# An RWKV attention fused into a cosine feed-forward: the end of the first order, the source of two chunks' bonus sums, the place of the decays' check and the lag of the last units

## The chip, the cores and the metric

One Trainium2 chip, one of its cores. The metric is device microseconds (us) of one execution; the profile is of one further execution of the same program.

## The reference, cut to what matters

```python
def _attn_ref(r, k, v, w, u):          # (4, 8, 768, 48) each, u (8, 48)
    for t in range(S):
        cur = einsum('bhd,bhe->bhde', u * k[t], v[t])
        y[t] = einsum('bhd,bhde->bhe', r[t], state + cur)
        state = w[t][..., None] * state + einsum('bhd,bhe->bhde', k[t], v[t])
def _moe_ref(x, w_in, w_out):          # x (3072, 384), w_in (384, 2048), w_out (2048, 384)
    h = x @ w_in
    return (h * cos(h)) @ w_out
```

The attention's output, with its heads side by side, is x.

## The kernel before, in words

**Tiling.** The sequence is cut into 24 chunks of 128 steps, numbered in the order of work: chunks 0 to 3 are the first chunk of each of the four batches, 4 to 7 the second, and so on. Two chunks make a block, so there are 12 blocks. The feed-forward of a block is 8 units (`NU`), each of two 128-wide pieces of the 2048. There are 96 units (`slots`), and t counts them. Blocks 0 and 1 share t = 0 to 15 in a mixed order; from t = 16 on, block 2 has t = 16 to 23, block 10 t = 80 to 87, block 11 t = 88 to 95.

**A unit.** `mm1(t)` is 18 matmuls on TensorE into a PSUM bank `ph`. Then comes the gate: I (ScalarE, L402), S (VectorE, L405), N (the sine on ScalarE, L418), M (VectorE, L419, the last reader of `ph`), H (ScalarE, the rounded high part, into `gs`), L (GpSimd, the low part, L145, in two halves). `mm2(t)` is 12 matmuls that read `gs` and add to the block's sums. `LAG` is 2: mm2(t-2) stands behind mm1(t). `gs` has two buffers, and while blocks 0 and 1 are both open `ph` has two banks (h0, h1) and all else on TensorE two (a0, a1).

**A block of attention.** For each chunk: loads (`load`, `lr` for r and k as they lie in memory, `lv`), the decay's two scans and products on VectorE (`decay`: e, f, r, k), the bonus sum (`diag`), which GpSimd's affine_select places on a diagonal (`asb`), the scores (`a`, written into `asb` by copy_predicated, P), the transposes of k (`t`, copied out as `kn`, K), the state (`s`, `d`), the own products (`o`), the products with the past (`p`) and their split into `xT` (X: xh on ScalarE, then x on VectorE), which mm1 of that block reads and which frees the two banks of `o`.

**Bonus sums.** Below chunk `BY_PE` VectorE multiplies r and k (`rkt`, L216), TensorE sums with u (`pc`, L241) and ScalarE copies (`cd`). From `BY_PE` on, `lr` loads r and k, two products are made (m, L247, and u, L248, with `u_sb`), and VectorE sums (c, L252). The engines of m and u come from a table: GpSimd in `EARLY`, VectorE in `LATER`. The buffers of `lr` ("h", two) are those through which the weights pass.

**Order.** `START` is the order for t = 0 to 15. There only TensorE runs in the order as written; the other engines' queues are put in order by a planner that works with estimated durations, and each queue then runs strictly in that order. From t = 16 on TensorE, VectorE, ScalarE and GpSimd run in the order of `PLAN`, whose row t % 8 is read for each t; only SP's queue is planned. `check_decays` (a load of 768 KB, a reduction and a maximum on VectorE) runs `WCH` = 6 times, behind the row of t = 90 to 95. `take_vote` stands behind t = 95: three small VectorE steps and two pairs of small matmuls (`pv`) in TensorE's queue. The program ends with a branch on the vote.

Of the kernel before, what the change touches and what calls it, by code (L numbers as in the profile page):

```python
# [26 lines left out]
NCB = 6  # L27
W129 = NP * 129
BLK = 2
BY_PE = 8  # L30
BT = BLK * C
WCH = 6
IN_PARTS = 2
# [12 lines left out]
LAG = 2  # L46
# [6 lines left out]
PLAN = ["t+2 t+3 load+6 mm1 K+2 K+3 e+4 I S k+4 N M mm2 H L f+4",  # L53
# [12 lines left out]
PAIR = "0001110101010101"  # L66
NEEDS = dict(decay="load", lr="load", lv="load", diag="lr", d="decay", a="decay diag", t="decay",
             o="a lv", s="t d lv", p="o d")
# [3 lines left out]
def rwkv_cos_ffn(ctx: ExitStack, tc: tile.TileContext, tr, tn, tv, u, ut, wts, w, rkw, vst, us, xs, out):  # L72
    nc = tc.nc
# [15 lines left out]
    def bank(kind, shape, name):  # L89

        tags = BANKS[stage[0]]
        turn[kind] += 1
        return ps.tile(shape, F32, tag=tags[kind][turn[kind] % len(tags[kind])], name=name)
# [3 lines left out]
    def buf(tag, shape, dtype, name=None, pool=sb):  # L97
        return pool.tile(shape, dtype, tag=tag, name=name or tag, bufs=BUFS.get(tag, 1))
# [31 lines left out]
    E = {}  # L130
# [49 lines left out]
    by_hand, parts = [False], {}  # L180
# [9 lines left out]
    def att_load(j):  # L190
# [8 lines left out]
        if j == 0:  # L199
            E["qt"].dma_start(out=u_by_head, in_=ut)  # L200
        if j == BY_PE:
            E["qt"].dma_start(out=u_sb, in_=u.to_broadcast([C, DM]))
# [9 lines left out]
    def att_decay(a):  # L212

        if a["j"] < BY_PE:
            a["rkt"] = buf("rkt", [R, NP, C], F32)
# [21 lines left out]
    def att_diag(a):  # L237
        if a["j"] < BY_PE:
            pc = bank("a", [C, 512], "pc")[:, :8]
            for p in range(NP):  # L240
                nc.tensor.matmul(out=pc[:, 2 * p:2 * p + 2], lhsT=a["rkt"][:, p], rhs=u_by_head[:, p], start=True, stop=True)  # L241
            cd = buf("cd", [C, 8], F32)
            copy("cd", cd, pc)
            picked(a, cd)
        else:
            rk = a["rk"][:, 0]
            part(("m", a["j"]), lambda: E["rk"].tensor_tensor(out=rk, in0=rk, in1=a["rk"][:, 1], op=ALU.mult))  # L247
            part(("u", a["j"]), lambda: E["ru"].tensor_tensor(out=rk, in0=rk, in1=u_sb, op=ALU.mult))  # L248

            def sums():  # L250
                cd = buf("cd", [C, 8], F32)
                nc.vector.tensor_reduce(out=cd, in_=rk.rearrange("p (h d) -> p h d", d=HD), axis=mybir.AxisListType.X, op=ALU.add)  # L252
                picked(a, cd)

            part(("c", a["j"]), sums)
# [131 lines left out]
    def check_decays(n):  # L387

        ww = buf("tt", [128, w.shape[1] // WCH], F32, "ww")
        nc.sync.dma_start(out=ww, in_=w[:, n * w.shape[1] // WCH:(n + 1) * w.shape[1] // WCH])  # L390
        top = buf("top", [128, 1], F32)
        nc.vector.tensor_reduce(out=top, in_=ww, axis=mybir.AxisListType.X, op=ALU.max, apply_absolute_value=True)
        nc.vector.tensor_tensor(out=wmax, in0=wmax, in1=top, op=ALU.max)
# [33 lines left out]
    def mm1(t, half=None):  # L427
        i, u = seq[t]
        if not half:
            weights("f", (u + 1) * FU + LEAD + FLEAD)  # L430
            weights("w", (u + 1) * FU + LEAD)
            for j in range(BLK):
                att(i * BLK + j, "x")
            units[t] = bank("h", [C, FU, BT], "ph")
        xT, ph = xts[i], units[t]
        for fi in range(FU) if half is None else (half,):
            n = 0
            for kt in range(KT):
                for a, b in PASSES:
                    nc.tensor.matmul(out=ph[:, fi], lhsT=wgt[u * FU + fi][:, 0, a, kt * 128:(kt + 1) * 128], rhs=xT[:, b, kt],  # L440
                                     start=n == 0, stop=n == 3 * KT - 1)
                    n += 1
        if half is None or half == FU - 1:
            gate(sb, ph, t)
# [35 lines left out]
    NU = NF // FU  # L480
# [3 lines left out]
    for i in PAIR:  # L484
# [3 lines left out]
    slots = len(seq)  # L488
    seen = set()
    n_checked = [0]  # L490
    done = {"f": 0, "w": 0}
    steps = dict(load=None, lr=att_load_rk, lv=att_load_v, decay=att_decay, diag=att_diag, d=att_dstate,
                 a=att_scores, t=att_transpose, s=att_state, o=att_own, p=att_past, x=att_x)

    def att(j, n):

        whole = n in "osp"
        if not 0 <= j < (NBLK if whole else NG) or (j, n) in seen:
            return
        for m in ("decay" if n == "diag" and j < BY_PE else NEEDS.get(n, "")).split():  # L500
            for c in (range(j * BLK, (j + 1) * BLK) if whole and m not in "osp" else (j,)):
                att(c, m)
        i = j // BLK
        if n == "load":
            for m in "osp":
                att((j - BUFS["tt"]) // BLK, m)
        elif n == "t":
            att((j - BUFS["kn"]) // BLK, "s")
        elif n == "d" and j >= NB:
            att(i - SAME, "s")  # L510
            att((j - BUFS["dd"]) // BLK, "s")
            att(i - 1, "p")
        elif n == "lv":
            att((j - BUFS["v"]) // BLK, "o")
            att((j - BUFS["v"]) // BLK, "s")
        elif n == "x":
            att(i, "p")
        seen.add((j, n))
        if n == "load":
            att_load(j)  # L520
        else:
            steps[n](j if whole else atts[j])
# [8 lines left out]
    def up(n):  # L531

        if n == 0 and up1[0] < slots:
            if up1[0] - up1[1] > LAG:
                up(1)
            mm1(up1[0])
            up1[0] += 1
        elif n == 1 and up1[1] < up1[0]:
            mm2(up1[1])
            up1[1] += 1  # L540

    def events(i, row, t):
        for e in row.split():
            n, _, d = e.partition("+")
            if e == "mm1":
                up(0)
            elif e == "mm2":
                if up1[1] <= t - LAG:
                    up(1)
            elif e in "ISNMHL":  # L550
                if (e, t) in parts:
                    parts.pop((e, t))()
            elif n in "efrkmucPKXn":
                at = i * (1 if n in "Xn" else BLK) + int(d)
                for m in dict(e=("decay",), m=("diag",)).get(n, ()):
                    att(at, m)
                if (n, at) in parts:
                    parts.pop((n, at))()
            else:
                att(i * (1 if n in "osp" else BLK) + int(d), n)  # L560

    def take_vote():
        vote = cst.tile([128, 1], F32, name="vote")
        nc.vector.tensor_single_scalar(out=vote, in_=wmax, scalar=1.0, op=ALU.is_gt)
        least = cst.tile([R, 1], F32, name="least")
        nc.vector.tensor_reduce(out=least, in_=wholes.rearrange("p g a -> p (g a)"), axis=mybir.AxisListType.X, op=ALU.min)
        low = cst.tile([R, 1], F32, name="low")
        nc.vector.tensor_single_scalar(out=low, in_=least, scalar=LEAST, op=ALU.is_le)
        pv = bank("a", [C, 512], "pv")
        nc.tensor.matmul(out=pv[:1, 0:1], lhsT=vote, rhs=ones[:, 0:1], start=True, stop=True)  # L570
        nc.tensor.matmul(out=pv[:1, 1:2], lhsT=ones[:R, 0:1], rhs=low, start=True, stop=True)
        votes = cst.tile([1, 1], F32, name="votes")
        nc.vector.tensor_reduce(out=votes, in_=pv[:1, 0:2], axis=mybir.AxisListType.X, op=ALU.add)
        nc.vector.tensor_copy(out=bad, in_=votes)
# [3 lines left out]
    up1 = [0, 0]  # L578
# [13 lines left out]
    engines(LATER)  # L592
    by_hand[0] = True
    with tc.manual_schedule(engines={ET.PE, ET.DVE, ET.Activation, ET.Pool}):
        for t in range(up1[0], slots + LAG):
            events(t // NU, PLAN[t % NU], t)
            if t >= slots - NU + 2 and n_checked[0] < WCH:
                check_decays(n_checked[0])
                n_checked[0] += 1
            if t == slots - 1:  # L600
                take_vote()
    assert not parts, list(parts)

    fast.close()
# [157 lines left out]
```

## Time and profile before

| | |
|---|---|
| median of the runs | 545.68 us |
| profiled execution, its own time | 545.42 us |
| its span, first to last instruction | 543.6 us |
| mean granted clock of TensorE | 0.972 |
| busy: TensorE matmul / weight load | 510.0 / 493.2 us |
| busy: VectorE / ScalarE / GpSimd | 378.3 / 274.1 / 213.5 us |
| HBM over the span | 93 GB/s |

The profiled execution stands 0.26 us below the median, and 1.8 us of its time lie outside its span. Busy shares are means over stages that differ: the weights and blocks 0 and 1 at the start, the even course of blocks 2 to 10, and block 11, which has no attention beside it.

### The profile page before, as it was taken

How to read it: one execution, taken by the hardware profiler on the slowest of the kernel's cores; microseconds unless marked ns; L12 is line 12 of the kernel's file. 1: busy time of each engine (PE TensorE's matmuls, PEld its weight loads, DVE VectorE, ACT ScalarE, POOL GpSimd, SP SyncE). 2: the span in 40 equal slices, each digit the busy share in tenths (PEclk: the TensorE clock that was granted, in tenths of full speed). 3: DMA queues.
4: the chain of work that ended last, by engine and by line, in shares of the span. 5: the costliest groups of instructions: out<-in, count | busy, mean ns of one | idle time of the engine just before them, and what ended most of it. 6: DMA issues, size and time to landing. Idle time of an engine off the chain costs nothing. (4 is left out here: it accounts for less than half of the span.)

```text
span 543.6 us, 11944 instructions
## 1 busy us (share of the span) xinstructions
PE 510.0 (94%) x4980; PEld 493.2 (91%) x4980; DVE 378.3 (70%) x568; ACT 274.1 (50%) x456; POOL 213.5 (39%) x274
## 2 busy tenths in 40 slices
PE   3667999989999999999999999999999999999995
PEld 3656898989999999999999999999999999999984
DVE  7998999954647947947947947947947847433682
ACT  1788999533444444444444444444444444444541
POOL 4161355743233533533533533533533634323331
PEclk9869999988999999999999999999999999999997
DMA  8984851105141150151150151151150130030200
GB/s 274 323 305 137 276 165 60 60 1 137 60 135 32 59 139 27 60 130 38 59 149 19 60 138 31 59 132 34 59 173 2 60 118 0 30 118 1 87 2 32
DMA packets 16440, 51.38 MB, mean 95 GB/s; under 512 B 1984, under 2 KB 8384, under 8 KB 16384
## 3 DMA queue, kind: packets, MB, share of 16 engines
q1 hardware_dynamic: 16240, 50.49, 30.3%
q8 instruction: 40, 0.66, 0.5%
q14 instruction: 16, 0.13, 0.1%
q10 hardware_dynamic: 144, 0.10, 0.1%
HBM read 45.87 MB, written 4.72 MB: 93 GB/s over the span
## 5 line engine op out<-in xcount | busy, mean ns | idle before, releaser
L145 POOL TENSOR_TENSOR gs<-rr,gs 128x256 fp32r<-128x256 f32 x192 | 160.0, 854 | 249.9 <-ACT gs L142 249.9
L440 PE MATMUL ph<-xT,w 128*128 128x256 f32 x1728 | 224.2, 283 | 6.4 <-ACT w L142 4.6
L440 PEld LDWEIGHTS ph<-xT,w 128*128 128x128 f32 x1728 | 215.5, 190 | 9.8 <-ACT w L142 5.1
L459 PE MATMUL acc<-w,gs 128*128 128x384 f32 x1152 | 221.2, 342 | 1.0 <-DVE rr L419 1.0
L459 PEld LDWEIGHTS acc<-w,gs 128*128 128x128 f32 x1152 | 199.9, 191 | 1.8 <-issue 1.4
L405 DVE SCALAR_TENSOR_TENSOR rr<-rr,ph 128x512 f32<-128x512 int32 x96 | 65.5, 683 | 90.9 <-ACT rr L402 90.4
L418 ACT ACTIVATE rr<-rr,quarter 128x512 f32<-128x512 f32 x96 | 69.4, 723 | 85.5 <-DVE rr L405 85.4
L142 ACT CAST gs<-rr 128x512 fp32r<-128x512 f32 x96 | 59.6, 620 | 63.1 <-DVE rr L419 42.4
L419 DVE TENSOR_TENSOR rr<-rr,ph 128x512 f32<-128x512 f32 x96 | 65.7, 684 | 30.2 <-ACT rr L418 30.2
L402 ACT ACTIVATE rr<-ph 128x512 int32<-128x512 f32 x96 | 57.4, 598 | 55.8 <-PE ph L440 55.2
L262 POOL TENSOR_SCALAR_AFFINE_SELECT asb<-cd 128x512 f32<-128x512 f32 x48 | 40.6, 868 | 65.1 <-DVE cd L252 40.9
L222 DVE TENSOR_TENSOR_SCAN ee<-tt,one_e 112x516 f32<-112x516 f32 x24 | 32.1, 1339 | 1.8 <-DMA tt<-tr 1.8
L289 DVE COPY_PREDICATED asb<-mask,pa 128x512 f32<-128x512 uint8 x48 | 31.8, 727 | 2.3 <-PE pa L285 2.3
L229 DVE TENSOR_TENSOR_SCAN tt<-tt,inj 112x516 f32<-112x516 f32 x24 | 30.6, 1276 | 0.6
L145 DVE TENSOR_TENSOR xT<-py,xT 128x384 fp32r<-128x384 f32 x24 | 12.2, 551 | 25.6 <-ACT xT L142 25.6
L285 PE MATMUL pa<-tt 48*128 48x128 f32 x384 | 29.1, 303 | 0.5 <-ACT ob L472 0.5
L285 PEld LDWEIGHTS pa<-tt 48*128 48x128 f32 x384 | 25.8, 208 | 3.6 <-issue 2.2
L241 PEld LDWEIGHTS pc<-u_by_head,rkt 112*128 112x128 f32 x64 | 11.1, 259 | 17.0 <-DVE rkt L216 8.6
L241 PE MATMUL pc<-u_by_head,rkt 112*128 112x2 f32 x64 | 11.4, 300 | 15.8 <-DVE rkt L216 13.4
L234 DVE TENSOR_TENSOR tt<-tt 112x512 f32<-112x512 f32 x24 | 21.6, 898 | 0.0
L142 ACT COPY past<-dd 48x192 f32<-48x192 f32 x40 | 14.0, 350 | 13.4 <-DVE dd L275 13.0
L235 DVE TENSOR_TENSOR tt<-tt,ee 112x512 f32<-112x512 f32 x24 | 19.1, 797 | 0.0
(65 smaller groups left out, 343.9 us busy)
## 6 DMA issues: line engine op xcount, KB each, us to landing
tt<-tr SPq DMA_DIRECT2D x22, 674.2 KB, 6.9
raw<-wts SPq DMA_DIRECT2D x16, 768.0 KB, 5.9
rk<-tn SPq DMA_DIRECT2D x16, 384.0 KB, 3.7
v<-tv SPq DMA_DIRECT2D x24, 224.0 KB, 5.8
ww<-w SPq DMA_DIRECT2D x6, 768.0 KB, 5.2
out<-ob SPq DMA_DIRECT2D x23, 192.0 KB, 2.0
tt<-tr SPq DMA_DIRECT2D x4, 224.0 KB, 4.6
tt<-tr SPq DMA_DIRECT2D x2, 226.2 KB, 3.6
```

Source lines behind the costliest of these rows:

```text
L142: (nc.scalar.copy if E[name] is nc.scalar else E[name].tensor_copy)(out=out, in_=in_)
L145: E[name].tensor_tensor(out=out, in0=full, in1=high.bitcast(F32), op=ALU.subtract)
L222: nc.vector.tensor_tensor_scan(out=ee.rearrange("p a t -> p (a t)")[:, ::-1], data0=wp[:, 1:W129 + 1][:, ::-1], data1=one_e.rearrange("p a ...
L262: nc.gpsimd.affine_select(out=asb, in_=col.unsqueeze(2).to_broadcast([C, NP, C]), pattern=[[0, 4], [1, C]], compare_op=ALU.is_equal, fill= ...
L285: nc.tensor.matmul(out=pa[h][:, p], lhsT=a["k3"][rows(h), p], rhs=a["r3"][rows(h), p], start=True, stop=True)
L289: nc.vector.copy_predicated(a["asb", h], mask, pa[h])
L402: nc.scalar.activation(made["rr"].bitcast(I32), ph, AF.Copy, scale=INV2PI / W_SCALE, bias=0.25)
L405: nc.vector.scalar_tensor_tensor(out=made["rr"], in0=made["rr"].bitcast(I32), scalar=-2.0 * math.pi * W_SCALE, in1=ph, op0=ALU.mult, op1=A ...
L418: N=lambda: nc.scalar.activation(made["rr"], made["rr"], AF.Sin, scale=1.0 / W_SCALE, bias=quarter),
L419: M=lambda: nc.vector.tensor_tensor(out=made["rr"], in0=made["rr"], in1=ph, op=ALU.mult), H=high, L=low)
L440: nc.tensor.matmul(out=ph[:, fi], lhsT=wgt[u * FU + fi][:, 0, a, kt * 128:(kt + 1) * 128], rhs=xT[:, b, kt], start=n == 0, stop=n == 3 * K ...
L459: nc.tensor.matmul(out=accs[i][j][:, :DM], lhsT=gs[:, a, fi, j * C:(j + 1) * C], rhs=wgt[u * FU + fi][:, 1, b], start=u == 0 and fi == 0 a ...
```

## The change

Five things. `BY_PE` falls to 6, so chunks 6 and 7 get their bonus sums from `lr` loads, m, u and c. The last row of `START` is put in another order: transposes of chunks 4 and 5, state of block 2, then its own products and those with the past, with a unit between each. At t = 18 a row of its own (`FIRST`) puts mm1 ahead of the scores of chunks 6 and 7. The decays' check goes to t = 82 to 87 and the vote behind t = 92. The last three units have rows of their own (`LAST`): mm1(94) and mm1(95) follow each other, mm2 lags by 3, H and L stand behind mm2 of the unit that frees their buffer, and L of units 94 and 95 is made by VectorE in one piece.

```diff
-BY_PE = 8
+BY_PE = 6
-         "mm2 m0 m1 o2 p2 mm2 x4 decay6 m0 m1 diag6 lv6 mm2 t4 t5 decay7 m0 m1 mm2 diag7 s2 lv7 lr8 lr9 load8 load9 d6 d7 lv8 lv9"]
+         "mm2 m0 m1 lr6 lr7 diag6 decay6 mm2 t4 t5 m0 m1 lv6 lv7 diag7 decay7 s2 mm2 o2 p2 load8 lr8 lr9 m0 m1 x4 mm2 load9 d6 d7 lv8 lv9"]
+FIRST = {2: "mm1 a+2 a+3 I S m+4 N M P+2 P+3 mm2 H L"}
+LAST = "mm1 I S N M", "mm1 I S N M mm2 h l", "mm2 h l"
+CHECK = 14
@@
-            if up1[0] - up1[1] > LAG:
+            if up1[0] - up1[1] > LAG + 1:
@@
-            elif e in "ISNMHL":
-                if (e, t) in parts:
-                    parts.pop((e, t))()
+            elif e in "ISNMHLhl":
+                at = (e.upper(), t - e.islower())
+                if at in parts:
+                    parts.pop(at)()
@@
-        for t in range(up1[0], slots + LAG):
-            events(t // NU, PLAN[t % NU], t)
-            if t >= slots - NU + 2 and n_checked[0] < WCH:
+        up2 = up1[0]
+        for t in range(up2, slots + LAG):
+            n = t % NU
+            if t == slots - 2:
+                E["g0"] = nc.vector
+            row = FIRST[n] if t < up2 + NU and n in FIRST else PLAN[n]
+            events(t // NU, row if t < slots - 2 else LAST[t - slots + 2] if t <= slots else "mm2", t)
+            if t >= slots - CHECK and n_checked[0] < WCH:
                 check_decays(n_checked[0])
                 n_checked[0] += 1
-            if t == slots - 1:
+            if t == slots - 4:
                 take_vote()
+        while up1[1] < slots:
+            up(1)
```

## Rows read from the trace of the kernel before

**Rows 1.** Windows: busy us and count of each engine, TensorE's clock, DMA, GB/s.
```profile
120.00:140.00 20.00, 19.76 (x154) 19.41 (x155) 9.60 (x16) 8.88 (x19) 6.85 (x10) 0.87 0.40 113
...
250.00:300.00 50.00, 50.00 (x495) 48.85 (x494) 35.80 (x58) 22.77 (x40) 19.75 (x27) 1.00 0.21 62
```

**Rows 2.** Timeline of TensorE, 108 to 142 us: start, us, instruction, idle before it.
```profile
108.90 0.64 PE L352 MATMUL py<-asb,v 128*32 128x128 f32 x16
...
111.82 2.37 PE L459 MATMUL acc<-w,gs 128*128 128x384 f32 x12
...
114.03 2.26 PE L440 MATMUL ph<-xT,w 128*128 128x256 f32 x18
...
118.23 1.86 PE L241 MATMUL pc<-u_by_head,rkt 112*128 112x2 f32 x8 [1.94 <-DVE xT L145]
...
119.96 4.19 PE L459 MATMUL acc<-w,gs 128*128 128x384 f32 x12
...
123.94 1.46 PE L298 MATMUL pt<-ident,tt 112*128 112x112 f32 x8
...
129.45 0.95 PE L241 MATMUL pc<-u_by_head,rkt 112*128 112x2 f32 x8
...
132.58 2.34 PE L440 MATMUL ph<-xT,w 128*128 128x256 f32 x18
...
141.73 2.43 PE L285 MATMUL pa<-tt 48*128 48x128 f32 x32 [0.53 <-ACT ob L472]
```

**Rows 3.** Timeline of the other engines, 96 to 118 us.
```profile
96.07 8.32 SPq L206 DMA_DIRECT2D rk<-tn  x2
...
107.29 2.61 POOL L145 TENSOR_TENSOR gs<-rr,gs 128x256 fp32r<-128x256 f32 x2 [1.94 <-ACT gs L142]
...
109.23 1.76 DVE L229 TENSOR_TENSOR_SCAN tt<-tt,inj 112x516 f32<-112x516 f32 x1
...
112.36 0.69 DVE L419 TENSOR_TENSOR rr<-rr,ph 128x512 f32<-128x512 f32 x1 [0.19 <-ACT rr L418]
...
116.59 0.62 ACT L142 CAST gs<-rr 128x512 fp32r<-128x512 f32 x1 [0.83 <-DVE rr L419]
...
117.11 0.85 ACT L142 CAST xT<-py 128x384 fp32r<-128x384 f32 x2
```

**Rows 4.** Windows of 2 us, columns as in the first group.
```profile
44.00:46.00 2.00, 0.66 (x18) 0.21 (x8) 2.00 (x4) 2.00 (x3) 0.00 (x0) 1.00 0.06 17
...
118.00:120.00 2.00, 1.77 (x9) 1.77 (x9) 1.23 (x3) 0.47 (x1) 0.70 (x2) 0.55 0.00 0
...
534.00:536.00 2.00, 2.00 (x8) 2.00 (x8) 0.00 (x0) 0.00 (x0) 0.00 (x0) 0.50 0.03 8
```

**Rows 5.** Groups by line: shapes, count, busy us, mean ns, idle before.
```profile
L392 DVE TENSOR_REDUCE top<-ww 128x1 f32<-128x1536 f32 x6 | 10.5, 1746 | 0.0
...
L252 DVE TENSOR_REDUCE cd<-rk 128x8 f32<-128x384 f32 x16 | 8.8, 549 | 0.3
...
L216 DVE TENSOR_TENSOR rkt<-tt 112x512 f32<-112x512 f32 x8 | 6.2, 779 | 0.0
```

**Rows 6.** Timeline of all engines, 526 to 540 us.
```profile
526.45 2.25 PE L459 MATMUL acc<-w,gs 128*128 128x384 f32 x12
...
532.53 0.15 DVE L564 TENSOR_SCALAR vote<-wmax 128x1 f32<-128x1 f32 x1
...
533.20 6.65 PE L459 MATMUL acc<-w,gs 128*128 128x384 f32 x24
```

**Rows 7.** Timeline of unit 85 in block 10, 482 to 489 us.
```profile
482.49 2.26 PE L440 MATMUL ph<-xT,w 128*128 128x256 f32 x18
...
485.48 0.69 DVE L405 SCALAR_TENSOR_TENSOR rr<-rr,ph 128x512 f32<-128x512 int32 x1 [2.08 <-ACT rr L402]
...
486.67 2.26 PE L440 MATMUL ph<-xT,w 128*128 128x256 f32 x18
...
486.95 0.69 DVE L419 TENSOR_TENSOR rr<-rr,ph 128x512 f32<-128x512 f32 x1 [0.79 <-ACT rr L418]
```

## The prediction

> **What bounds the kernel now.** First the table of windows over the span. From 250 to 300 us TensorE is busy for all 50.00 us at clock 1.00, and VectorE for 35.80 [rows 1]: the even course is TensorE's, and an edit there gains only what it takes from TensorE. Its reserves lie where it waits or runs at half clock. Two such places touch the change. From 120 to 140 us the mean clock is 0.87 [rows 1]; the other place is the end. So the second view is TensorE's timeline at these places, the third the windows of 2 us for the clock.
>
> At the first place the reader is to see the sums of chunk 6 (`pc`) begin at 118.23 after 1.94 us of idleness, put down to VectorE's `xT` [rows 2]. That is a bank: with two banks for all but gates and sums, `pc` needs one of those in which block 2's own products lie, and X frees them. The products end before 111.82, where mm2(11) begins [rows 2], but X begins at 117.11, since ScalarE's queue has it behind H of unit 13 at 116.59 [rows 3]. Behind the wait the clock is 0.55 [rows 4]; mm2(12) takes 4.19 us instead of the 2.37 of mm2(11) [rows 2].
>
> At the end mm2(93) begins at 526.45, and mm2(94) and mm2(95) only at 533.20: in between TensorE's queue holds the vote's matmuls, and the vote begins at 532.53 [rows 6], behind the last check. Then the 24 matmuls take 6.65 us [rows 6] at clock 0.50 [rows 4].
>
> **The change part by part.** All sums are against the profiled execution (545.42 us, span 543.6); the median is 0.26 us above it.
>
> *First order's end.* The pitch of mm1 and mm2 together is 486.67 - 482.49 = 4.18 us [rows 7], so 2.09 each. What falls away between 108.90, where block 2's own products begin, and mm1(16) at 132.58 [rows 2]:
> - the wait ahead of `pc`: 118.23 - (114.03 + 2.09) = 2.11 us;
> - `pc` of chunk 6: 119.96 - 118.23 = 1.73 us;
> - mm2(12) at half clock: 123.94 - 119.96 = 3.98 instead of 2.09, 1.89 us;
> - the eight transposes at half clock, 1.46 us [rows 2]; at full clock half, so some 0.6 us in the queue (an estimate);
> - `pc` of chunk 7, 0.95 us [rows 2], some 0.9 in the queue.
>
> Together 7.2 us. What comes instead: the products (2.9 us, 108.90 to 111.82) no longer stand between mm1(13) and mm2(11). TensorE now comes to mm1(14) at 108.90 + 2.09 + 0.7 for the transposes = 111.7, and mm1(14) needs the bank of unit 12, whose M begins at 112.36 and ends at 113.05 [rows 3]: a new wait of 1.3 us. Net 5.9 us. Behind it there is room: the state, mm2(12) and the products (2.1 + 2.9 us for the latter two) stand between mm1(14) and mm1(15), and mm1(15) and mm2(13) (4.2 us) between the products and the transposes of chunks 6 and 7, which need X. X then has no late H in front: unit 13's is at 116.59, the products now end near 121.
>
> *Bonus sums.* VectorE loses two `rkt`, 2 x 0.78, and gets two sums, 2 x 0.55 [rows 5]: 0.5 us less. But in `START` m and u are GpSimd's, four instructions of 384 columns. The trace has no such instruction; its nearest row is L with two of 256 columns in 2.61 us [rows 3], so 1.3 to 2 us each, some 6 us, in GpSimd's queue ahead of or between the Ls. Their loads can go no earlier than those of chunks 8 and 9 now: the second of these is issued at 96.07 + 8.32 = 104.39 [rows 3], behind the last weights, which hold the buffer. From below, all this hides in GpSimd's idle times (1.94 us ahead of 107.29 alone [rows 3]) and M of unit 12 comes 0.5 to 1.5 us earlier; from above, M comes 2 us later. I take no shift, as both signs have a row. SP's queue holds `lr8` and `lr9` behind the sums that free their buffers, and behind them the loads of chunk 9, which is wanted only some five units later.
>
> *t = 18.* The scores of chunks 6 and 7 waited 0.53 us for a bank [rows 2]; with mm1(18) ahead that is covered. Gain 0.5 us.
>
> *Check.* A reduction of 1.75 us [rows 5] and a maximum of one column, six times, in VectorE's queue between M and the next S. The maximum lies between 0.15, the vote's step of one column [rows 6], and the 0.69 of a whole M [rows 7]. S of unit 85 stands after 2.08 us of idleness [rows 7], so each check pushes the next S by at most 1.75 + 0.69 - 2.08 = 0.36 us, 2.2 us in all. M(85) ends at 487.64, and its bank is wanted by mm1(87) at 486.67 + 4.18 = 490.85 [rows 7]: 3.2 us of room. So it costs nothing; without that room, up to 2.2 us. At t = 82 four P's stand in the same queue, but there the scores lengthen TensorE's part too. Loads for the check wait in SP's queue with no other load behind them.
>
> *Vote.* Behind t = 92 it stands after M(92). By rows 7, M begins 0.28 us after the next mm1 could; 0.69 for M and 533.20 - 532.53 = 0.67 from the vote to the next matmul [rows 6] make it some 1.6 us late. TensorE waits that long once. Its clock should hold: from 44 to 46 us it was busy for 0.66 of 2.00 us and the clock stayed 1.00 [rows 4].
>
> *Last units.* Gone: 533.20 - (526.45 + 2.09) = 4.66 us of wait, and 6.65 - (2 x 2.09 + 0.16) = 2.31 us of half clock. With lag 3, H(95) waits for mm2(93) and has the 2.09 us of mm2(94) for its own 0.62 [rows 3] and for L on VectorE, which I put at M's 0.69: covered. Net of the vote's wait, 5.4 us.
>
> Sum: 5.9 + 0.5 + 5.4 = 11.8 us; 545.42 - 11.8 = 533.6, and against the median **533.9 us**.
>
> **Rivals.**
> *The gate of unit 12 comes later than now.* M(12) slips by 0.7 us or more, the wait ahead of mm1(14) passes the 1.94 us behind which the clock fell [rows 2], and half clock follows. For it: VectorE is saturated there, and a scan took 1.76 us at 109.23 [rows 3] while L ran on GpSimd. Against it: 0.5 us less VectorE work. Price: a wait of 2.5 us instead of 1.3 and some 3 us of clock (1.89 + 0.6 and part of a unit, as now), so 533.9 + 4.2 = 538.1.
> In its hard form each m and u stops VectorE for its whole length, 6 us; less the 0.5, M comes 5.5 us later, and with the clock's 3 us the time is 533.9 + 8.5 = 542.4. This is what the Trainium skill's page "SBUF — State Buffer", section "Who interferes with whom", would make of it: a VectorE instruction with two SBUF inputs and a GpSimd one that reads SBUF share a port, and the second to issue waits for the first to end. The rows neither bear it out nor rule it out: that scan began at 109.23, when L had 0.67 us to go.
> *X is late again.* The planner puts xh behind another gate, and the wait moves ahead of the transposes of chunks 6 and 7, with the clock behind it: 2.1 + 3 us less, 539.
> *Slower than before.* The two `lr` loads take both "h" buffers before the last two weights do. Then the weights wait for m, u and c, and mm1(14) for the weights of the last unit. It turns slower when that wait exceeds 1.3 + 11.8 - 3 = 10.1 us; with 6 us for m and u and the 8.3 us in which a weight passes its buffer now [rows 3] it is some 14 us, and the time 549.6. Against it: the loads stand behind all weights in `START`.
> *The vote's wait halves the clock* as the longer one does now: 2.3 + some 1 us of it again, 537.
>
> **How the numbers follow.** The forecast 0.60; the gate's late form 0.17, its hard form 0.05; late X 0.09; the vote's clock 0.06; slower 0.03. The range runs from no wait ahead of mm1(14) and 1 us more from earlier waits that shrink with VectorE's load (545.68 - 13.1 - 1.0, near 531.5) to the late forms with a further microsecond, 540; left out are the hard form, the slower case and tails. Two per cent, about what a measurement of this kernel tells from no change, is 534.8: the forecast's own spread (531.5 to 536) has some 0.47 of its 0.60 below that. So faster 0.47, same 0.51, and slower 0.02, since part of the slower case stays within 2%.
>
> **What would show it.** mm1(16) near 126.7 instead of 132.58, no `pc` after chunk 5, and one wait of about 1.3 us ahead of mm1(14) at clock 1.00. The pair of `pv` at t = 92 with 1 to 1.6 us around it. After mm1(95) four mm2 without a gap at clock 1.00, and the last matmul some 11.8 us earlier. No gap in t = 82 to 88. I am wrong if a window between 108 and 127 us shows clock 0.5, if TensorE waits ahead of mm1(14) or t6 for over 2 us, or if `pv` is followed by a low clock.

## The result, and the profile after

The changed kernel takes 538.88 us (median; 538.74 to 538.94), the kernel before 545.54 us beside it: a ratio of 0.9895, with a 95% interval of 0.9867 to 0.9922. One run of the kernel before took 1260.72 us, and the ratio, which is of the fast runs, leaves it out. The gain is 6.7 us by the medians and some 5.7 us by the ratio; 11.8 us were forecast. The time lies inside the stated range of 531.5 to 540 us, but in the part of it that belonged to the rivals. Line numbers are 3 higher than before: M is L422, mm1 L443, mm2 L462, the products m and u L250 and L251, their sum c L255.

The profiled execution took 538.93 us, 6.49 us less than that of before. Its end first. TensorE's timeline of the kernel after:

```profile
513.05 2.25 PE L462 MATMUL acc<-w,gs 128*128 128x384 f32 x12
...
516.24 0.19 PE L574 MATMUL pv<-ones,vote 128*1 128x1 f32 x2 [0.94 <-DVE vote L568]
...
516.70 2.37 PE L443 MATMUL ph<-xT,w 128*128 128x256 f32 x18
...
521.00 4.36 PE L443 MATMUL ph<-xT,w 128*128 128x256 f32 x36
525.20 8.49 PE L462 MATMUL acc<-w,gs 128*128 128x384 f32 x48
```

The reader is to see the last 36 + 48 matmuls without a gap, 8.49 us for 48 where 24 took 6.65 us before [rows 6]. The last ends at 533.69; before it was 533.20 + 6.65 = 539.85 [rows 6]. Of these 6.16 us, 0.84 were already there when block 11 began: its own products start at 474.42 instead of 475.26. So the end is worth 5.3 us. The vote costs 516.70 - (513.05 + 2.09) = 1.56 us, once.

Then the first order's end. TensorE's timeline, 105 to 144 us:

```profile
108.42 2.34 PE L443 MATMUL ph<-xT,w 128*128 128x256 f32 x18 [1.17 <-DVE rr L422]
110.59 2.92 PE L462 MATMUL acc<-w,gs 128*128 128x384 f32 x12
113.36 0.93 PE L301 MATMUL pt<-ident,tt 112*128 112x112 f32 x8
117.48 2.36 PE L443 MATMUL ph<-xT,w 128*128 128x256 f32 x18 [3.19 <-DVE rr L422]
120.46 0.67 PE L323 MATMUL pst<-v,kn 128*64 128x48 f32 x16 [0.62 <-ACT kn L145]
121.90 0.67 PE L323 MATMUL pst<-v,kn 128*64 128x48 f32 x16 [0.78 <-ACT kn L145]
...
132.71 2.35 PE L443 MATMUL ph<-xT,w 128*128 128x256 f32 x18
...
143.36 2.06 PE L288 MATMUL pa<-tt 48*128 48x128 f32 x32
```

All that was to go is gone: no `pc` of chunks 6 and 7 and no half clock (below). Yet mm1(16) stands at 132.71, where it was at 132.58 [rows 2]. mm1(14) begins at 117.48, 4.4 us behind the 113.05 at which the forecast's new wait was to end. In place of what went there are four waits, 1.17 + 3.19 + 0.62 + 0.78 = 5.8 us, and mm2(11), which holds TensorE until 113.36, 0.7 us beyond its 2.09. The two long waits are put down to M (L422). Windows of the kernel after, columns as in rows 1:

```profile
100.00:120.00 20.00, 15.35 (x113) 13.88 (x110) 13.24 (x18) 6.22 (x12) 12.34 (x13) 1.00 0.21 61
120.00:140.00 20.00, 18.76 (x248) 17.91 (x249) 11.47 (x20) 10.76 (x22) 8.87 (x12) 1.00 0.40 114
...
450.00:500.00 50.00, 50.00 (x466) 48.98 (x466) 35.98 (x47) 22.30 (x37) 16.53 (x24) 1.00 0.16 56
```

From 100 to 120 us TensorE works for 15.35 of 20 us, VectorE for only 13.24: the engine on which M runs is not full, it stands. The row of 450 to 500 us, where the check now lies, is full for TensorE. VectorE's timeline says at what it stands:

```profile
104.38 0.55 DVE L255 TENSOR_REDUCE cd<-rk 128x8 f32<-128x384 f32 x1 [2.03 <-POOL rk L251]
...
108.20 1.22 DVE L225 TENSOR_TENSOR_SCAN ee<-tt,one_e 112x516 f32<-112x516 f32 x1
111.35 0.55 DVE L255 TENSOR_REDUCE cd<-rk 128x8 f32<-128x384 f32 x1 [1.93 <-POOL rk L251]
111.82 0.17 DVE L230 RECIPROCAL inj<-ee 112x4 f32<-112x4 f32 x1
111.91 1.48 DVE L238 TENSOR_TENSOR tt<-tt,ee 112x512 f32<-112x512 f32 x1
113.31 1.22 DVE L232 TENSOR_TENSOR_SCAN tt<-tt,inj 112x516 f32<-112x516 f32 x1
114.57 0.69 DVE L237 TENSOR_TENSOR tt<-tt 112x512 f32<-112x512 f32 x1
115.18 0.68 DVE L408 SCALAR_TENSOR_TENSOR rr<-rr,ph 128x512 f32<-128x512 int32 x1
116.65 0.69 DVE L422 TENSOR_TENSOR rr<-rr,ph 128x512 f32<-128x512 f32 x1 [0.79 <-ACT rr L421]
```

Each of the two new sums c waits about 2 us for its product u. Behind the second stand, in a queue that runs in order, k, f and r of chunk 7 and then S(12) at 115.18, and so M(12), at 116.65 instead of 112.36 [rows 3]. And GpSimd's timeline, why the products are late:

```profile
99.16 3.09 POOL L265 TENSOR_SCALAR_AFFINE_SELECT asb<-cd 128x512 f32<-128x512 f32 x2
102.22 1.03 POOL L250 TENSOR_TENSOR rk<-rk 128x384 f32<-128x384 f32 x1
103.33 1.02 POOL L251 TENSOR_TENSOR rk<-rk,u_sb 128x384 f32<-128x384 f32 x1
...
108.25 1.98 POOL L250 TENSOR_TENSOR rk<-rk 128x384 f32<-128x384 f32 x1 [1.79 <-DMA rk<-tn]
110.31 1.01 POOL L251 TENSOR_TENSOR rk<-rk,u_sb 128x384 f32<-128x384 f32 x1
```

The first pair stands behind two selects that take 3.09 us, the second behind its load, which is issued at 105.0, behind the first sum: SyncE waited 5.3 us for it. And the selects are slow here: 1.18 and 1.95 us, against a median of 0.64 us over all 48 (duration in ns, least, median and most; then SyncE's wait between 90 and 114 us, in all, times, longest):

```profile
L265 POOL TENSOR_SCALAR_AFFINE_SELECT asb<-cd x48: 628/638/1968, 9.1 to 460.7; 128x512 f32<-128x512 f32 x48
```
```profile
SPq L209 <- DVE cd L255: 5.3, 1, 5.3
```

So the theory: the end is right; at the start the cause is the place of the two sums in VectorE's queue, ahead of the gate that frees mm1(14)'s bank, with producers that come late. Rivals: the amount of work that m, u and c bring (a sum would cost the same anywhere near); the new order of TensorE itself, whatever makes the sums; for t = 18, that its wait is hidden anyway.

### The profile page after: what moved, and what is told of

It is laid out like the page before. It is cut to its first block, busy times and chain, and to the rows that moved or that the text cites. A ratio compares the mean times of both kernels' runs of the same rounds, so it can differ in the third digit from the quotient of the medians.

```text
span 537.2 us, 11909 instructions
## 1 busy us (share of the span) xinstructions
PE 503.7 (94%) x4964; PEld 485.7 (90%) x4964; DVE 378.9 (71%) x570; ACT 274.2 (51%) x454; POOL 212.9 (40%) x274
## 4 chain that ended last, share of the span: by engine, by line
PE 77%; DVE 13%; ACT 4%; issue 2%; POOL 2%; DMA 1%; DVEq 0%; ACTq 0%; POOLq 0%
PE ph L443 33%; PE acc L462 32%; PE pa L288 4%; DVE h L173 2%; PE py L355 2%; DVE w L148 2%; PE py L360 2%; PE pst L323 2%; DVE rr L422 1%; DVE ee L225 1%; DVE tt L232 1%; PE py L374 1%; DVE rr L408 1%; PE pt L301 1%; DVE tt L237 1%
## 5 line engine op out<-in xcount | busy, mean ns | idle before, releaser
L148 POOL TENSOR_TENSOR gs<-rr,gs 128x256 fp32r<-128x256 f32 x188 | 155.1, 846 | 245.4 <-ACT gs L145 245.4
L443 PE MATMUL ph<-xT,w 128*128 128x256 f32 x1728 | 224.4, 284 | 11.5 <-ACT w L145 5.2
L443 PEld LDWEIGHTS ph<-xT,w 128*128 128x128 f32 x1728 | 215.2, 190 | 15.6 <-ACT w L145 5.6
L462 PE MATMUL acc<-w,gs 128*128 128x384 f32 x1152 | 217.3, 338 | 1.1 <-DVE rr L422 1.0
L462 PEld LDWEIGHTS acc<-w,gs 128*128 128x128 f32 x1152 | 195.9, 188 | 2.5 <-issue 1.2
L422 DVE TENSOR_TENSOR rr<-rr,ph 128x512 f32<-128x512 f32 x96 | 65.7, 684 | 29.1 <-ACT rr L421 29.0
L265 POOL TENSOR_SCALAR_AFFINE_SELECT asb<-cd 128x512 f32<-128x512 f32 x48 | 42.8, 915 | 60.4 <-DVE cd L255 40.9
L244 PEld LDWEIGHTS pc<-u_by_head,rkt 112*128 112x128 f32 x48 | 8.3, 262 | 14.7 <-DVE rkt L219 8.4
L244 PE MATMUL pc<-u_by_head,rkt 112*128 112x2 f32 x48 | 8.7, 303 | 13.5 <-DVE rkt L219 12.9
L237 DVE TENSOR_TENSOR tt<-tt 112x512 f32<-112x512 f32 x24 | 21.0, 875 | 0.1
L238 DVE TENSOR_TENSOR tt<-tt,ee 112x512 f32<-112x512 f32 x24 | 20.0, 835 | 0.0
```

What stands on the lines that cost most here:

```text
L148: E[name].tensor_tensor(out=out, in0=full, in1=high.bitcast(F32), op=ALU.subtract)
L265: nc.gpsimd.affine_select(out=asb, in_=col.unsqueeze(2).to_broadcast([C, NP, C]), pattern=[[0, 4], [1, C]], compare_op=ALU.is_equal, fill= ...
L422: M=lambda: nc.vector.tensor_tensor(out=made["rr"], in0=made["rr"], in1=ph, op=ALU.mult), H=high, L=low)
L462: nc.tensor.matmul(out=accs[i][j][:, :DM], lhsT=gs[:, a, fi, j * C:(j + 1) * C], rhs=wgt[u * FU + fi][:, 1, b], start=u == 0 and fi == 0 a ...
```

## The experiments

The kernel before gave medians of 543.4 to 544.6 us beside these runs (541.4 to 546.6 in single runs), so ratios are against those. All kernels here compute the whole of the reference.

**The end alone.** The kernel before with the check, the vote and `LAST` of the change:

```diff
-BY_PE = 6
+BY_PE = 8
-         "mm2 m0 m1 lr6 lr7 diag6 decay6 mm2 t4 t5 ... load9 d6 d7 lv8 lv9"]
+         "mm2 m0 m1 o2 p2 mm2 x4 decay6 m0 m1 diag6 ... d6 d7 lv8 lv9"]
-FIRST = {2: "mm1 a+2 a+3 I S m+4 N M P+2 P+3 mm2 H L"}
+FIRST = {}
```

> The kernel before with only the check in block 10, the vote behind t = 92 and the rows for the last units. If the end is worth what the trace of after shows at its place (last matmul 6.16 us earlier, 0.84 of that already there at block 11's own products), it gives 5.3 us: 540.2. If part of the end's gain came from the changed start (clock, phases), it gives clearly less, 542 or more.

538.65 us, 0.9884 (0.9838 to 0.9929) against 544.38: 5.7 us less, as much as the whole change brings by its ratio.

**The start alone.** The change without `LAST`, with check and vote where they were:

```diff
-CHECK = 14
+CHECK = 6
-            if t == slots - 2:
-                E["g0"] = nc.vector
-            events(t // NU, row if t < slots - 2 else LAST[t - slots + 2] if t <= slots else "mm2", t)
+            events(t // NU, row, t)
-            if t == slots - 4:
+            if t == slots - 1:
```

> The kernel after with the end put back: the check at t = 90 to 95, the vote behind t = 95, lag 2. Both theories of the lost gain expect the start alone to be worth under 1.5 us, 544 to 545.5. The forecast's own terms (5.9 + 0.5 us) would give 539.

544.35 us, 0.9999 (0.9974 to 1.0024): nothing. The two parts add up. Its wait ahead of mm1(14) is that of the change to the hundredth, but in this profile half clock follows (timeline, then a window):

```profile
117.21 3.53 PE L443 MATMUL ph<-xT,w 128*128 128x256 f32 x18 [3.19 <-DVE rr L422]
```
```profile
118.00:120.00 2.00, 2.00 (x12) 2.00 (x11) 0.89 (x2) 1.24 (x3) 1.29 (x2) 0.50 0.00 0
```

**The sums on TensorE again.** The new order, but the bonus sums of chunks 6 and 7 as before:

```diff
-BY_PE = 6
+BY_PE = 8
-         "mm2 m0 m1 lr6 lr7 diag6 decay6 ...
+         "mm2 m0 m1 diag6 decay6 ...
```

> The kernel after with BY_PE back at 8 and without the two early loads of r and k: the new order, but the bonus sums of chunks 6 and 7 by TensorE again. Theory of the sums (VectorE stands for 2.0 and 1.9 us at the two sums until GpSimd's products come, and S of unit 12 is queued behind): the waits ahead of mm1(13) and most of that ahead of mm1(14) go, 4.3 less some 1.3 us, against 1.8 us of sums on TensorE: 537 to 537.5, with mm1(14) at 113 to 114. Rival, theory of the order (TensorE comes to mm1(14) too early, whoever makes the sums): the wait ahead of mm1(14) stays over 2.5 us and the time is 539.5 to 541.

536.5 us, 0.9863 (0.9817 to 0.9909; single runs 535.56 to 537.98), a little better than either theory said. M(12) is at 112.46, so the new order itself doesn't delay the gate. What TensorE waits for is a bank, freed by the copy of `pc` (timelines of VectorE, then of TensorE):

```profile
112.46 0.69 DVE L422 TENSOR_TENSOR rr<-rr,ph 128x512 f32<-128x512 f32 x1 [0.19 <-ACT rr L421]
```
```profile
114.48 0.60 PE L301 MATMUL pt<-ident,tt 112*128 112x112 f32 x4 [2.02 <-ACT cd L145]
114.86 2.35 PE L443 MATMUL ph<-xT,w 128*128 128x256 f32 x18
```

So the second source of the sums does remove a wait of 2 us, and puts a longer one in its place: as the change has it, the new source costs some 2.4 us more than the old one.

**The sums by hand.** Chunks 6 and 7 still by VectorE, but out of the planner's part: all three steps on VectorE, written out at t = 16 and 17, behind mm1 of those units, with the loads `lr8` and `lr9` behind them:

```diff
-         "mm2 m0 m1 lr6 lr7 diag6 decay6 ... lv7 diag7 decay7 s2 mm2 o2 p2 load8 lr8 lr9 m0 ...
-FIRST = {2: "mm1 a+2 a+3 I S m+4 N M P+2 P+3 mm2 H L"}
+         "mm2 m0 m1 lr6 lr7 decay6 ... lv7 decay7 s2 mm2 o2 p2 load8 m0 ...
+FIRST = {0: "t+2 t+3 load+6 mm1 K+2 K+3 m+2 u+2 c+2 lr+4 e+4 I S k+4 N M mm2 H L f+4",
+         1: "mm1 m+3 u+3 c+3 lr+5 I S r+4 N M mm2 H L",
+         2: "mm1 a+2 a+3 I S m+4 N M P+2 P+3 mm2 H L"}
```

> The kernel after with m, u and c of chunks 6 and 7 at t = 16 and 17 on VectorE, in the written order, instead of in the planned start; the loads stay. Theory of the sums: S of unit 12 is no longer behind a waiting sum, M(12) ends by 113, mm1(14) waits 0 to 1.3 us, mm1(16) begins near 128 instead of 132.7, 534 to 535.5. Theory of the order: the wait ahead of mm1(14) stays over 2.5 us, 537.5 to 539.

535.21 us, 0.9835 (0.9793 to 0.9877). Timeline of TensorE, then of VectorE:

```profile
112.32 2.35 PE L445 MATMUL ph<-xT,w 128*128 128x256 f32 x18
115.22 0.67 PE L325 MATMUL pst<-v,kn 128*64 128x48 f32 x16 [0.55 <-ACT kn L147]
116.66 0.67 PE L325 MATMUL pst<-v,kn 128*64 128x48 f32 x16 [0.78 <-ACT kn L147]
...
127.45 2.35 PE L445 MATMUL ph<-xT,w 128*128 128x256 f32 x18
```
```profile
109.93 0.68 DVE L410 SCALAR_TENSOR_TENSOR rr<-rr,ph 128x512 f32<-128x512 int32 x1
111.40 0.69 DVE L424 TENSOR_TENSOR rr<-rr,ph 128x512 f32<-128x512 f32 x1 [0.79 <-ACT rr L423]
```

S(12) comes 5.25 us earlier than in the change, and mm1(14) doesn't wait at all. The waits for `kn` stay, 1.33 us here and 1.40 in the change: they don't come from the place of the sums (with `pc` on TensorE ahead of the state, as in the run before, they are covered). And the move isn't free: from mm1(16) to block 3's own products, which begin at 147.66, it takes 20.21 us here and 19.10 in the change.

**The sums written later.** The place of `diag6` and `diag7` in the row is changed, to behind mm1(15), and `lr8` and `lr9` follow them:

```diff
-         "mm2 m0 m1 lr6 lr7 diag6 decay6 mm2 t4 t5 m0 m1 lv6 lv7 diag7 decay7 s2 mm2 o2 p2 load8 lr8 lr9 m0 m1 x4 mm2 ...
+         "mm2 m0 m1 lr6 lr7 decay6 mm2 t4 t5 m0 m1 lv6 lv7 decay7 s2 mm2 o2 p2 load8 m0 m1 x4 diag6 diag7 lr8 lr9 mm2 ...
```

> The kernel after with the bonus sums of chunks 6 and 7 written behind mm1(15) in START; the loads stay where they are. The planner still puts both sums ahead of S of unit 12 in VectorE's queue, but behind the second scan and the last product of chunk 7, when GpSimd's products should be there. Theory of the sums (what costs is standing at them, not their work): VectorE waits under 0.5 us at them, the 1.17 us ahead of mm1(13) go, M(12) ends near 114 and mm1(14) waits 1 to 2.5 us: 535.5 to 537. Theory of the order: no change, 538.5 to 539.

537.68 us, 0.9868 (0.9826 to 0.991), between the two ranges. The expectation that VectorE would wait under 0.5 us did not hold. The planner still puts both sums ahead of S(12); the first now finds its product there, the second waits (VectorE's timeline, then TensorE's):

```profile
102.82 2.06 DVE L225 TENSOR_TENSOR_SCAN ee<-tt,one_e 112x516 f32<-112x516 f32 x1
...
113.61 0.55 DVE L255 TENSOR_REDUCE cd<-rk 128x8 f32<-128x384 f32 x1 [2.29 <-POOL rk L251]
114.08 0.68 DVE L408 SCALAR_TENSOR_TENSOR rr<-rr,ph 128x512 f32<-128x512 int32 x1
```
```profile
116.38 3.90 PE L443 MATMUL ph<-xT,w 128*128 128x256 f32 x18 [2.32 <-DVE rr L422]
```

With one standing of 2.29 us left of two, S(12) is 1.1 us earlier and so is mm1(14).

**The products on VectorE.** Row and places as in the change; only m and u go to VectorE, which gets more work by four instructions of 0.55 us:

```diff
-EARLY = dict(... rk="p", ru="p", ...)
+EARLY = dict(... rk="v", ru="v", ...)
```

> The kernel after with m and u of chunks 6 and 7 on VectorE in START instead of GpSimd. VectorE has 4 x 0.55 us more, but waits for no GpSimd; it still has to wait for the second load of r and k, which lands near 108. If the wait for GpSimd's products is the cause, mm1(14) comes 1 to 3 us earlier than in after, 536 to 538. If the cause is VectorE's amount of work in this stretch, it comes later, 539.5 to 541.

535.37 us, 0.9829 (0.9787 to 0.9871), better than was expected. VectorE's timeline, then TensorE's:

```profile
106.93 0.56 DVE L250 TENSOR_TENSOR rk<-rk 128x384 f32<-128x384 f32 x1 [0.21 <-DMA rk<-tn]
107.41 0.55 DVE L255 TENSOR_REDUCE cd<-rk 128x8 f32<-128x384 f32 x1
...
112.97 0.66 DVE L422 TENSOR_TENSOR rr<-rr,ph 128x512 f32<-128x512 f32 x1
```
```profile
113.77 2.34 PE L443 MATMUL ph<-xT,w 128*128 128x256 f32 x18 [1.51 <-DVE rr L422]
```

VectorE has 2.2 us more to do and M(12) is 3.7 us earlier, mm1(16) at 128.99. That decides against the rival of the amount of work: what cost the time is that VectorE stood for another engine. It doesn't tell why that engine was late, since m and u are off GpSimd here and can neither stand in its queue nor be slowed beside VectorE. (The planner orders this kernel's queues anew; r of chunk 7 also falls behind M(12).)

**The vote in two parts.** The vote's three VectorE steps ahead of the row of t = 88, its matmuls behind that of t = 89:

```diff
+            if t == slots - NU:
+                weigh()          # the three VectorE steps, taken out of take_vote
-            if t == slots - 4:
+            if t == slots - NU + 1:
```

> The kernel after with the vote's three VectorE steps ahead of the row of t = 88 and its matmuls behind t = 89, when the steps are long done. By rows of after, the pair of vote matmuls costs 516.70 - 515.14 = 1.56 us, all of it standing behind M(92): the wait goes and some 0.2 us stay, 537.5. If TensorE loses the same elsewhere (ScalarE and VectorE set the pace of the last units), 538.9 stays.

538.21 us (537.41 to 539.93), 0.9889 (0.9842 to 0.9936): the time can't tell it from the change. The timeline can:

```profile
500.29 2.25 PE L462 MATMUL acc<-w,gs 128*128 128x384 f32 x12
502.47 0.19 PE L579 MATMUL pv<-ones,vote 128*1 128x1 f32 x2
...
502.64 2.37 PE L443 MATMUL ph<-xT,w 128*128 128x256 f32 x18
```

The vote costs 502.64 - (500.29 + 2.09) = 0.26 us instead of 1.56.

**The three together.** The sums by hand, the vote in two parts, the state of block 2 behind mm2(12), and at t = 18 the scores of chunk 7 behind mm2(16):

```diff
-         "... decay7 s2 mm2 o2 p2 ...
+         "... decay7 mm2 s2 o2 p2 ...
-FIRST = {2: "mm1 a+2 a+3 I S m+4 N M P+2 P+3 mm2 H L"}
+         2: "mm1 a+2 I S m+4 N M P+2 mm2 a+3 P+3 H L"}
```

> The kernel with the sums by hand, with the split vote (1.4 us), with the state of block 2 behind mm2(12), so that it does not wait for the copies of the transposes (0.55 + 0.78 us), and with the scores of chunk 7 behind mm2(16) (0.46 us). If these waits end the same chain, 535.2 - 3.2 = 532; if one is replaced by the next wait (own products for the state's bank), 533 to 533.5.

532.9 us (532.78 to 533.23), 0.9782 (0.9741 to 0.9824): it beats both kernels. Putting the state later gained nothing; its two waits only became one ahead of the own products, at clock 1.00 (timeline):

```profile
119.86 0.43 PE L357 MATMUL py<-asb,v 128*32 128x128 f32 x8 [1.79 <-DVE sn L334]
```

mm1(16) is at 127.58, no earlier than with the sums by hand alone (127.45). The 2.0 us between these two profiles are the vote (1.3) and the scores: block 3's own products begin at 147.09 instead of 147.66.

**t = 18 as before, and the change once more** (side by side):

```diff
-FIRST = {2: "mm1 a+2 a+3 I S m+4 N M P+2 P+3 mm2 H L"}
+FIRST = {}
```

> The kernel after without the row FIRST: at t = 18 the scores of chunks 6 and 7 stand ahead of mm1(18) again. The forecast's term is 0.5 us, the wait of the scores for a bank: 0.5 us more than the kernel after in the same call, and a wait of about 0.5 us ahead of the scores in the trace. Rival: the wait is hidden anyway in this order, and there is no difference.

> The kernel after unchanged, as the measure for the runs of the same call: 538 to 539.5, with the wait ahead of mm1(14) near 3.2 us again. If its clock falls behind that wait, as it did in the start alone, up to 3 us more.

538.85 us, 0.9932 (0.9907 to 0.9957), and 538.9 us, 0.9921 (0.9895 to 0.9947): no difference. From mm1(16) to block 3's own products it takes 151.64 - 132.45 = 19.19 us without the row of its own and 151.81 - 132.71 = 19.10 with it (profile of the change). Without it the scores of chunks 6 and 7 show no wait in the timeline:

```profile
141.00 2.14 PE L288 MATMUL pa<-tt 48*128 48x128 f32 x32
```

The wait was hidden anyway, once the order ahead of it was changed. The repeated change shows something else (timeline, window):

```profile
117.34 4.18 PE L443 MATMUL ph<-xT,w 128*128 128x256 f32 x18 [3.20 <-DVE rr L422]
...
133.60 2.35 PE L443 MATMUL ph<-xT,w 128*128 128x256 f32 x18
```
```profile
118.00:120.00 2.00, 2.00 (x11) 2.00 (x11) 0.76 (x2) 1.25 (x3) 1.42 (x2) 0.50 0.00 0
```

The same program, the same wait, and here half clock behind it: mm1(16) is 0.9 us later than in the change's first profile, and this profiled execution took 539.94 us, 1.0 us more.

## Why the prediction was wrong, point by point

**The end was right.** Forecast 5.4 us net, found 5.3; the vote's wait 1.6 forecast, 1.56 found, and the clock held. `end_alone` gives 5.7 us by itself.

**The check was right.** Its six reductions took 1.75 us each and the maxima 0.565, between the two bounds; TensorE was busy for 50.00 us of 450 to 500. That it was the named room of 3.2 us on the bank that covered the check is argued, not shown.

**What the first order's end removes went, but its size was that of one profile.** `end_alone` has the old start, and there the five terms come to some 5.5 us instead of 7.2, as the half clock was shorter (`pc` of chunk 6 takes 0.92 us in the queue and mm2(12) 3.72, instead of 1.73 and 3.98). Where VectorE doesn't stand for GpSimd, the sequence comes out near the forecast: with the products on VectorE the wait ahead of mm1(14) is 1.51 us (1.3 forecast), and with the sums by hand mm1(16) is at 127.45 (126.7 forecast). That the latter is so near is in part luck, as two misses cancel (below).

**The step that failed is "I take no shift, as both signs have a row".** M(12) came 4.3 us later, beyond its upper bound of 2. That made mm1(14) 4.4 us late, of the 6.0 us by which mm1(16) missed its 126.7. The durations of m, u and the sum were not at fault: m and u took 1.01 to 1.98 us (1.3 to 2 forecast), the sum 0.55. Missing was the question that the edit called for: where do the two c stand in VectorE's in-order queue, when is their product ready by GpSimd's queue and by the load, and who is behind them. c gained a producer on another engine; at 2.03 and 1.93 us these waits are 3.96 of the 4.3. The first moved M(11) and so mm1(13) (1.17 us), both together M(12) and mm1(14) (3.19). The price of m and u was sought in GpSimd's queue, where it had cover but for the 0.7 us that mm2(11) waited for L; the rest was paid by who waited for them. The trace of before held most of it: the load of chunk 7 goes no earlier than some 104 (104.39 is where that issue ends; it begins at 104.1); with the 3.1 us that such loads take to land in the trace after (median) and m and u as forecast, the sum could not begin before some 110 to 111, while chunk 7's scan ran at 109.23 [rows 3]. A sum placed ahead of that scan had to stand.

Why the products were late has a second half, which no run separates: GpSimd was slowed beside VectorE. Together the two selects took 1.8 us more than twice their median, and m of chunk 7 0.95 us more than that of chunk 6. Without that, by an estimate from these rows, the first sum would have stood some 0.2 us instead of 2.03, and the second 1.0 us or less, as its load would have gone earlier too. The trace of before shows the same: L took 2.61 us [rows 3] beside two scans, and 1.44 at 113.86, with only S beside it, which reads PSUM.

**A wait that had no term.** The state waits 0.62 + 0.78 us for the copies `kn` of the transposes just ahead of it: with the new order one unit stands between the transposes and the state. With the sums by hand mm1(14) doesn't wait, so mm1(16) should have come 1.3 us ahead of the forecast's 126.7; it came 0.75 behind it, and 1.33 of these 2.05 us are the waits for `kn`. Moving the state only moved them.

**t = 18 was mis-sized:** 0.5 us forecast, 0.1 found, since the wait that it was to cover was no longer there. From mm1(16) to block 3's own products the kernel before took 152.66 - 132.58 = 20.08 us; 0.9 us of it is gone even without the row of its own, by the order ahead of it.

**The rivals.** The late gate is what happened: M(12) slipped, for a cause that was not the one given (a standing queue, not a full one). Its price of 538.1 us is near the measured time by luck: the wait was 3.19 us instead of its 2.5, and its 3 us of clock were not paid, as in the change's first profile the clock is 1.00 throughout this stretch. Where the clock did fall behind the same wait, it cost 0.9 us at most: mm1(16) is at 132.43 in the start alone and at 133.60 in the repeated change, instead of 132.71. While TensorE works at half speed the copies `kn` get ready, and their 1.4 us of wait are gone. The hard form, 6 us of VectorE lost to m and u, has nearly the right size (M 5.5 us late, 4.3 found) and the wrong victim: the two engines did slow each other, but it was mostly GpSimd that lost, and VectorE paid by waiting. At the second m, VectorE's scan had begun 0.05 us before it and took its 1.22 us, while m took 1.98 instead of 1.03; in `sums_later` m began 0.05 us before the scan, and there m took 1.02 and the scan 2.06. So in both overlaps the one that came second lost, 0.95 and 0.84 us. The Trainium skill says on its page "SBUF — State Buffer", section "Who interferes with whom", that issue order decides which of the two blocks; by that rule alone VectorE's loss in the change would have been nothing at this scan, and the trace agrees. X was not late, and the vote's clock held. The last weight's low part was made at 104.85 instead of 103.09, behind the first sum, but no wait of TensorE is put down to it.

**Open.** How much of the difference between the profiles of before and after at the start is clock: `end_alone`, whose start is that of before, has the same wait, 1.93 us ahead of `pc`, but its shorter half clock (above) has mm1(16) at 131.43 and not at 132.58. What part of the two sums' standing is GpSimd's slowing beside VectorE was estimated above, not tried. That the planner would place the sums well with better estimates of m, u and their loads was not tried.

## What to carry to other kernels

When an edit gives an instruction a producer on another engine, price the wait and not only the work: find its place in its own in-order queue, when the producer can be ready by that engine's queue and by its load, and which gate is queued behind. More work in one queue (2.2 us more on VectorE) can beat the same work spread over two engines, because nobody stands for it. Here the terms that only took a known idle stretch away at the end, with its half clock, came out within a few tenths (5.4 us forecast, 5.3 and 5.7 found); terms that rest on a queue that a planner will order anew need that order worked out first, or the steps written out by hand.

## What the runs showed of the hardware

- TensorE's clock is not settled by the program: behind the same wait of 3.2 us it stayed at 2.4 GHz in one profile of the changed kernel and fell to 1.2 GHz in another (1.00 and 0.50 in 118 to 120 us), while before it was 0.55 behind a wait of 1.94 us [rows 2, 4]. The kernel after, first profile:

```profile
118.00:120.00 2.00, 1.84 (x16) 1.64 (x14) 0.69 (x1) 1.24 (x4) 1.44 (x2) 1.00 0.00 0
```

- A product of 128x384 takes GpSimd 1.02 us and VectorE 0.55. Where a scan on VectorE and such a product on GpSimd began 0.05 us apart, the second lost 0.95 us (the product, in the change) or 0.84 us (the scan, in `sums_later`). u of chunk 6 in `sums_later`, which began beside that scan and ended beside a product on VectorE, took 2.74 us.
- A select of 128x512 on GpSimd takes 0.64 us (median); beside VectorE's steps with two operands in SBUF (L237, L238 and L173, at 99 to 102 us) two of them took 1.18 and 1.95 us.
